# Six of sixteen attention groups transposed by the vector engine and SBUF-to-SBUF DMAs instead of the tensor engine, the last output tile in two halves, and a new written order

## The chip, the cores and the metric

The kernel runs on one core of one Trainium2 chip. A core has a tensor engine (PE, with PEld for its weight loads), a vector engine (DVE), a scalar engine (ACT), a GpSimd (POOL) and a sync engine (SP), which here issues the DMAs. SBUF is the on-chip memory, PSUM the memory into which PE writes its sums; "bank" means one 512-column fp32 buffer of PSUM. The metric is the device time of one execution in microseconds. Before the change it is 413.14 us, the median of three runs (412.8 to 413.42).

## The reference

Inputs are q, k, v of shape (8 batches, 8 heads, 576 rows, 64) and p of shape (8, 8, 32, 64), then w_in (512 x 1024), conv_w (3 x 1024) and w_out (1024 x 512).

```
p_packed = sm_attn(p, k, v)              # first attention: 32 packed rows look at 576 rows
attn     = sm_attn(q, p_packed, p_packed) # second attention: 576 rows look at the 32
x   = attn, heads side by side            # (8, 576, 512)
h   = relu(x @ w_in)
c   = conv_w[0]*h[s-1] + conv_w[1]*h[s] + conv_w[2]*h[s+1]
out = (h * sigmoid(c)) @ w_out            # (8, 576, 512)
```

sm_attn(q, k, v) is softmax(q k^T / 8) v, with each row's maximum taken off first.

## The kernel before

**Tiling.** Four heads of a batch make a group; there are 16 groups, g = 0 to 15, two for each batch. First attention of a group: eight small matmuls (L444, `big<-kT,pT`) make a 128 x 576 tile of scores (4 heads x 32 packed rows on partitions, the 576 rows in columns); DVE takes the maximum (L487, `nm`); ACT makes the exponentials `a1` (L491; the profile calls it `a`). The product with v contracts over the 576 rows, so `a1` has to be turned: five PE transposes (L498, `big<-ident,a`) of 128 x 128 into PSUM and one ACT copy (L501, `a1T<-big`) into SBUF. Then 20 pairs of small matmuls (L507, `sm<-v,a1T`) give the packed result, which ACT scales (`pb`), PE transposes (L523) and ACT copies (`ppT`). Second attention scores the 576 rows against it (L444, `big<-qT,ppT`), DVE does the softmax (L531 to L561) and leaves `a2`.

**The rest.** packed_weight multiplies the packed result into w_in beforehand (L581), so that ffn1 (L633, 12 matmuls of 288 columns for each of 8 blocks of a batch) goes from `a2` straight to h. ACT and DVE then do relu, convolution and gate (L645 to L661). ffn2 makes the 36 output tiles of 128 rows: ACT and DVE split a tile into a high and a low part (`xhi` L671, `xlo` L674), then 8 steps of 3 matmuls of 512 columns (L716) add into one PSUM bank, ACT copies it (L721, `o`) and SP stores it (L723). The bank is `fo`; for tiles 31, 33 and 35 it is `sm`, so that the last five tiles alternate.

**What sets the order.** Each stream of work (a group's attention, a tile's ffn2) is a generator that yields steps: an engine, an expected duration, the buffers taken and given. The string `ORDER` is a written-out list of stream numbers; `flow.run` takes the next step of the named stream each time. So the order of instructions on each engine's queue is fixed by `ORDER`, and every engine works its own queue strictly in that order, waiting on semaphores where data or buffers are not ready. The durations in the steps serve only to decide how many filler matmuls (L244, `idle`) PE gets in its first waits. `a1` and `a1T` have one buffer each, `o` two. DMAs of SP rotate over eight semaphores (DMAHW0 to DMAHW7): the ninth waits until the first has landed.

The steps that the change touches are in `attention(g)`: `yield Step("PE", 544, take=["big", "a1T"], give=["a1"])`, the ACT step behind it, the PE step of L507; and in `ffn2(m)`, the eight PE steps and the store.

Of the kernel before, what the change touches and what calls it, by code (L numbers as in the profile page):

```python
# [185 lines left out]
def tile_packed_attention_conv_gate(  # L186
# [11 lines left out]
    nc = tc.nc  # L198
# [20 lines left out]
    HALVED = 4  # L219

# [20 lines left out]
    def warm(n):  # L241
# [5 lines left out]
        dict(kq=3, v=2, kT=1, qT=1, big=3, sm=1, fo=1, a1=1, a1T=1, pm=2, pT=2, pb=2, ppT=5, s2=2, a2t=1, a2=4)  # L247
# [232 lines left out]

    def attention(g):
# [12 lines left out]
        yield Step("PE", 544, take=["big", "a1T"], give=["a1"], cols=1280)  # L494
        t = big().rearrange("r f s -> r (f s)")
        for si in range(SV + 1):
            rows = a1[:, : 128 * SV].rearrange("c (r s) -> c s r", s=SV)[:, si, :] if si < SV else a1[:, S - 128 :]
            nc.tensor.transpose(out=t[:, si * 128 : (si + 1) * 128], in_=rows, identity=ident)  # L498
        yield Step("ACT", 584, give=["big"])
        a1T = wk.tile([128, SV + 1, 128], F32, name="a1T", tag="a1T", bufs=1)  # L500
        nc.scalar.copy(out=a1T.rearrange("r s n -> r (s n)"), in_=t[:, : (SV + 1) * 128])  # L501
        yield Step("PE", 737, after=[("v", g)], take=["sm"], give=["a1T", "v"], cols=960, tiled=True)
        t = small()
        for si in range(SV + 1):
            r = 0 if si < SV else 128 - TAIL
            for h in range(HG):
                nc.tensor.matmul(  # L507
                    out=t[32 * h : 32 * h + 32, :D],
                    lhsT=a1T[r:, si, 32 * h : 32 * h + 32],
                    rhs=G["v"][r:, head(g, h), si, :],  # L510
                    start=si == 0,
                    stop=si == SV,
                    tile_position=(r, 32 * h),
                    skip_group_check=True,
                )
# [150 lines left out]
    split = {}  # L666

# [13 lines left out]
    def ffn2(m):  # L681
# [16 lines left out]
        for c in range(NJ):  # L698
            after = [("w", 4 + c // 2)]
            if c == 0 and m:  # L700
                after.append(("fo", m - 1))
            if c == last:
                after.append(("x", m))
            yield Step(
                "PE",
                699,
                after=after,
                take=[bank] if c == 0 else (),
                give=["x"] if c == NJ - 1 else (),
                sets=[("fo", m)] if c == NJ - 1 else None,  # L710
                cols=1536,
            )
            if c == 0:
                t = small(bank)
            for i, (x, w) in enumerate(((hi, wo_hi), (hi, wo_lo), (lo, wo_hi))):
                nc.tensor.matmul(  # L716
                    out=t, lhsT=x[:, c, :], rhs=w[:, c, :], start=c + i == 0, stop=c == NJ - 1 and i == 2
                )
        yield Step("ACT", 478, take=["o"], give=[bank])
        o = wk.tile([128, DM], F32, name="o", tag="o")  # L720
        nc.scalar.copy(out=o, in_=t)  # L721
        yield Step("SP", 728, give=["o"])
        nc.sync.dma_start(out=out.rearrange("b s f -> (b s) f")[m * 128 : (m + 1) * 128, :], in_=o)  # L723
# [57 lines left out]
```

## Time and profile before

| what | value |
|---|---|
| median of three runs | 413.14 us |
| the profiled execution, its own time | 412.19 us |
| its span, first to last instruction | 410.4 us |
| granted TensorE clock | 0.999 |
| PE busy | 399.8 us, 97% |
| DVE busy | 335.2 us, 82% |
| ACT busy | 277.5 us, 68% |
| PE transposes of `a1` (L498) | 80, in 16 groups of 5 |
| ACT copies `a1T` (L501) | 16, 700 ns each |
| output stores (L723) | 36 of 256 KB, 2.3 us from issue to landing |

Matmuls are pipelined: a row's duration runs from its start to its modelled end and overlaps the next. What a matmul costs PE is the distance from its start to the next start. A row with "x5" is five instructions merged. "[0.67 <-ACT o L721]" behind a row says that the engine was idle for 0.67 us before it, until that instruction released it.

### The profile page before, as it was taken

The numbers are of one execution on the slowest core, as the hardware profiler recorded it, in microseconds if no ns is written. First come the engines' busy times: TensorE is split into PE (matmuls) and PEld (weight loads), VectorE is DVE, ScalarE is ACT, GpSimd is POOL, SyncE is SP. The second block draws the span as 40 slices with busy tenths as digits, with TensorE's granted clock in tenths as the row PEclk, the third lists the DMA queues.
The fourth block names the chain that finished last, engine by engine and source line by source line (L and its number), as shares of the span: only waits on it lengthen the run. The fifth ranks groups of instructions, "written<-read, shape, count | busy, mean of one in ns | idle before, by whom it ended". The sixth has DMA issues, their size and how long they took to land.

```text
span 410.4 us, 8121 instructions
## 1 busy us (share of the span) xinstructions
PE 399.8 (97%) x3335; PEld 320.5 (78%) x3335; DVE 335.2 (82%) x482; ACT 277.5 (68%) x480; POOL 1.6 (0%) x13
## 2 busy tenths in 40 slices
PE   6899999999999999999999998999999999999996
PEld 5668675877868787887788786878788878887884
DVE  0599999999999999999979998888996786657220
ACT  4799999977666686677666674675755667655221
POOL 1000000000000000000000000000000000000000
PEclk9999999999999999999999999999999999999999
DMA  7999999998659919733631093710100101101021
GB/s 280 382 342 353 180 283 163 153 117 163 106 114 198 174 53 124 159 84 83 112 65 21 3 181 81 130 49 4 53 26 2 51 0 53 51 2 51 27 77 51
DMA packets 135620, 47.21 MB, mean 115 GB/s; under 512 B 119700, under 2 KB 127892, under 8 KB 135584
## 3 DMA queue, kind: packets, MB, share of 16 engines
q1 hardware_dynamic: 135552, 46.67, 52.0%
q8 instruction: 26, 0.43, 0.5%
q14 instruction: 10, 0.08, 0.1%
q0 software_dynamic: 32, 0.02, 0.0%
HBM read 37.25 MB, written 9.44 MB: 114 GB/s over the span
## 4 chain that ended last, share of the span: by engine, by line
PE 90%; DMA 4%; ACT 2%; DVE 1%; SPq 1%; issue 0%; DVEq 0%; ACTq 0%
PE fo L716 44%; PE big L633 24%; PE sm L716 4%; PE big L444 4%; PE big L581 3%; DMA v<-in_v_dram 3%; PE sm L507 3%; PE big L498 2%; PE big L328 2%; DMA q<-in_q_dram 1%; PE idle L244 1%; PE big L428 1%; SPq L405 1%; PE sm L523 1%; PE big L597 1%; ACT kT L434 0%
## 5 line engine op out<-in xcount | busy, mean ns | idle before, releaser
L716 PE MATMUL fo<-wo_hi,xhi 128*128 128x512 f32 x264 | 108.1, 410 | 0.7 <-ACT o L721 0.7
L716 PE MATMUL fo<-wo_hi,xlo 128*128 128x512 f32 x264 | 104.5, 396 | 0.0
L716 PE MATMUL fo<-wo_lo,xhi 128*128 128x512 f32 x264 | 103.9, 393 | 0.0
L651 DVE SCALAR_TENSOR_TENSOR hgt<-hbuf,cw,hgt 128x576 f32<-128x576 f32 x64 | 51.6, 810 | 16.8 <-ACT hgt L649 16.7
L645 ACT ACTIVATE hbuf<-big 128x576 f32<-128x576 f32 x64 | 41.7, 654 | 33.4 <-PE big L633 33.0
L716 PEld LDWEIGHTS fo<-wo_hi,xhi 128*128 128x128 f32 x264 | 49.6, 188 | 17.1 <-issue 3.5
L674 DVE TENSOR_TENSOR xlo<-hgt,xhi 128x1024 fp32r<-128x1024 f32 (+1 forms) x44 | 44.7, 1021 | 21.3 <-ACT xhi L671 21.0
L716 PEld LDWEIGHTS fo<-wo_hi,xlo 128*128 128x128 f32 x264 | 49.6, 188 | 12.3
L716 PEld LDWEIGHTS fo<-wo_lo,xhi 128*128 128x128 f32 x264 | 49.7, 188 | 8.6
L633 PE MATMUL big<-a2hi,ghi 128*128 128x288 f32 x256 | 55.3, 297 | 0.0
L633 PE MATMUL big<-a2hi,glo 128*128 128x288 f32 x256 | 54.3, 294 | 0.0
L633 PE MATMUL big<-a2lo,ghi 128*128 128x288 f32 x256 | 54.2, 293 | 0.0
L661 DVE SCALAR_TENSOR_TENSOR hgt<-hgt,hbuf 128x576 f32<-128x576 f32 x64 | 47.4, 749 | 7.3 <-ACT hgt L659 6.9
L655 DVE SCALAR_TENSOR_TENSOR hgt<-hbuf,cw,hgt 128x576 f32<-128x576 f32 x64 | 51.4, 811 | 0.5
L659 ACT ACTIVATE hgt<-hgt 128x576 f32<-128x576 f32 x64 | 43.1, 686 | 12.6 <-DVE hgt L655 12.2
L649 ACT ACTIVATE hgt<-hbuf,cw 128x576 f32<-128x576 f32 x64 | 49.4, 778 | 0.6
L633 PEld LDWEIGHTS big<-a2hi,ghi 128*128 128x128 f32 x256 | 43.1, 188 | 5.2 <-ACT hbuf L645 0.8
L671 ACT CAST xhi<-hgt 128x1024 fp32r<-128x1024 f32 (+1 forms) x44 | 38.9, 889 | 11.1 <-PE fo L716 6.4
L721 ACT COPY o<-fo 128x512 f32<-128x512 f32 x33 | 19.4, 587 | 33.6 <-PE fo L716 33.2
L633 PEld LDWEIGHTS big<-a2lo,ghi 128*128 128x128 f32 x256 | 40.9, 188 | 0.0
L633 PEld LDWEIGHTS big<-a2hi,glo 128*128 128x128 f32 x256 | 40.8, 188 | 0.0
L487 DVE TENSOR_REDUCE nm<-big 128x1 f32<-128x576 f32 x16 | 12.0, 752 | 10.7 <-PE big L444 10.6
(90 smaller groups left out, 503.7 us busy)
## 6 DMA issues: line engine op xcount, KB each, us to landing
out_dram<-o SPq DMA_DIRECT2D x36, 256.0 KB, 2.3
v<-in_v_dram SPq DMA_DIRECT2D x16, 512.0 KB, 5.4
k<-in_k_dram SPq DMA_DIRECT2D x48, 144.0 KB, 4.3
q<-in_q_dram SPq DMA_DIRECT2D x48, 144.0 KB, 4.2
hgt<-in_moe_w_in_dram SPq DMA_DIRECT2D x3, 1024.0 KB, 11.7
hgt<-in_moe_w_out_dram SPq DMA_DIRECT2D x3, 1024.0 KB, 8.5
hgt<-in_k_dram SPq DMA_DIRECT2D x2, 576.0 KB, 6.6
hgt<-in_q_dram SPq DMA_DIRECT2D x2, 576.0 KB, 9.3
```

The lines of the kernel that those rows point to most:

```text
L444: nc.tensor.matmul(out=o.rearrange("c (j r) -> c j r", r=NR) if by_block(g) else o, lhsT=lhs[r, 32 * i : 32 * i + 32], rhs=rhs[r, :, h, :] ...
L633: nc.tensor.matmul(out=t[:, hf, :SH], lhsT=w[:, gg, js], rhs=x[:, hf * SH : (hf + 1) * SH], start=n == 0, stop=n == 3 * NG - 1,)
L645: nc.scalar.activation(out=h[:, 1 : S + 1].rearrange("c (f s) -> c f s", f=2), in_=t[:, :, :SH], func=AF.Relu, scale=0.5)
L649: nc.scalar.activation(out=d, in_=h[:, 1 : S + 1], func=AF.Copy, scale=cw[:, NJ + j : NJ + j + 1])
L651: nc.vector.scalar_tensor_tensor(out=d, in0=h[:, 0:S], scalar=cw[:, j : j + 1], in1=d, op0=ALU.mult, op1=ALU.add)
L655: nc.vector.scalar_tensor_tensor(out=d, in0=h[:, 2 : S + 2], scalar=cw[:, 2 * NJ + j : 2 * NJ + j + 1], in1=d, op0=ALU.mult, op1=ALU.add)
L659: nc.scalar.activation(out=d, in_=d, func=AF.Tanh)
L661: nc.vector.scalar_tensor_tensor(out=d, in0=d, scalar=1.0, in1=h[:, 1 : S + 1], op0=ALU.add, op1=ALU.mult)
L671: nc.scalar.copy(out=hi[:, js, o], in_=src[:, js])
L674: nc.vector.tensor_tensor(out=lo[:, js, o], in0=src[:, js], in1=hi[:, js, o].bitcast(F32), op=ALU.subtract)
L716: nc.tensor.matmul(out=t, lhsT=x[:, c, :], rhs=w[:, c, :], start=c + i == 0, stop=c == NJ - 1 and i == 2)
L721: nc.scalar.copy(out=o, in_=t)
```

## The change

For the groups g = 10 to 15 (`MOVED = 10`) the five PE transposes and the ACT copy are replaced. DVE turns the 128 x 576 exponentials in blocks of 32 x 32 with two instructions, one over 128 x 512 and one over 128 x 64, into one of two buffers that are halves of `stage` (the buffer that held raw weights at the start). A block is then transposed in itself but lies in the wrong place: rows of head h lie on partitions 32h to 32h+31, and should lie on the partitions of their quarter q of the 576 rows. Sixteen DMAs on SP's queue, one for each q and h, each 32 rows of 160 elements (640 B a row), move them inside SBUF to `a1T`, whose layout becomes (h, s, n) for all groups. The last output tile (m = 35) is summed in two halves of 256 columns, 24 matmuls each, in the same bank `sm`, and each half is copied and stored by itself. `ORDER` is a new list throughout.

```
@@ ORDER = (
-    "003m043k0302040304033l053u040b0b05060b083v3s0106060c3k0g0j060c07063q0j050c0j3t063k070c05063k3v0e3v063t0k3t060e0k"
+    "003m3k04033s0403020403040b06080c3t063k3l063t0b0c3u010g0705050b070j3k0c3k3q0c06050e3t060e063v06060k0506063v0a0k09"
...
+    afree = [stage[:, i * (SV + 1) * 128 : (i + 1) * (SV + 1) * 128] for i in range(2)]
...
     def attention(g):
...
-        yield Step("PE", 544, take=["big", "a1T"], give=["a1"], cols=1280)
...
+        if g >= MOVED:
+            yield Step("DVE", 760, after=[("wp", 2), ("wp", 5)], take=["ad"], give=["a1"])
+            blocks = afree.pop(0)
+            moved = blocks.rearrange("r (q s n) -> r q s n", q=4, s=SV + 1)
+            main = a1[:, : 128 * SV].rearrange("c (q r s) -> c q s r", q=4, s=SV)
+            nc.vector.transpose(out=moved[:, :, :SV, :], in_=main)
+            rest = a1[:, 128 * SV :].rearrange("c (q r) -> c q r", r=32)
+            nc.vector.transpose(out=moved[:, 4 - TAIL // 32 :, SV, :], in_=rest)
+            yield Step("SP", 1100, take=["a1T"], give=["ad"], parts=4 * HG)
+            a1T = wk.tile([128, SV + 1, 128], F32, name="a1T", tag="a1T", bufs=1).rearrange("r s n -> r (s n)")
+            a1T = a1T.rearrange("r (h s n) -> r h s n", h=HG, s=SV + 1)
+            for q in range(4):
+                for h in range(HG):
+                    nc.sync.dma_start(
+                        out=a1T[32 * q : 32 * q + 32, h].rearrange("r s n -> r (s n)"),
+                        in_=moved[32 * h : 32 * h + 32, q].rearrange("r s n -> r (s n)"),
+                    )
+            afree.append(blocks)
+        else:
 ...
-                    lhsT=a1T[r:, si, 32 * h : 32 * h + 32],
+                    lhsT=a1T[r:, h, si, :],
...
     def ffn2(m):
...
-        for c in range(NJ):
+        parts = 2 if m == NTT - 1 else 1
+        for n in range(NJ * parts):
+            q, c = divmod(n, NJ)
+            fs = slice(q * DM // parts, (q + 1) * DM // parts)
...
-                    out=t, lhsT=x[:, c, :], rhs=w[:, c, :], start=c + i == 0, stop=c == NJ - 1 and i == 2
+                    out=t[:, fs], lhsT=x[:, c, :], rhs=w[:, c, fs], start=c + i == 0, stop=c == NJ - 1 and i == 2
...
-        yield Step("ACT", 478, take=["o"], give=[bank])
+        yield from store(m, fs, bank)
+
+    def store(m, fs, bank=None):
+        yield Step("ACT", 45 + (fs.stop - fs.start) * 85 // 100, after=[("fo", m, fs.start * 2 // DM)], take=["o"], give=[bank] if bank else ())
         o = wk.tile([128, DM], F32, name="o", tag="o")
+        nc.scalar.copy(out=o[:, fs], in_=sums_of[m][:, fs])
+        yield Step("SP", 100 + (fs.stop - fs.start) * 123 // 100, give=["o"])
+        nc.sync.dma_start(out=out.rearrange("b s f -> (b s) f")[m * 128 : (m + 1) * 128, fs], in_=o[:, fs])
...
+    flow.add(store(NTT - 1, slice(0, DM // 2)))
```

In the changed kernel's line numbers L445 is the scores, L490 the maximum, L502 and L504 are the two DVE transposes, L510 the sixteen DMAs, L530 the product with v, L656 ffn1, L745 ffn2's matmuls, L753 its copy, L755 its store.

Counted over the whole program PE has 50 transposes of `a` where it had 80, 48 matmuls of 256 columns for the last tile where it had 24 of 512, and 38 filler matmuls where it had 39; all other counts on PE are as before.

**DVE around the transposes of group 14.** Before, on DVE, from the maximum of group 14 on:

```order
L487 TENSOR_REDUCE nm<-big 128x1 [waits PE_49]
L655 SCALAR_TENSOR_TENSOR hgt_76<-hbuf_79,cw,hgt_76 128x576 [waits DVE_49]
L548 RECIPROCAL sm_2911<-sm_2911 128x18
L531 STREAM_TRANSPOSE s_2979<-big 128x576 [waits PE_49]
L674 TENSOR_TENSOR xlo<-hgt_77,xhi 128x1024 [waits Activation_49]
```

Now:

```order
L490 TENSOR_REDUCE nm<-big 128x1 [waits PE_49]
L684 SCALAR_TENSOR_TENSOR hgt_76<-hgt_76,hbuf_80 128x576 [waits Activation_49]
L678 SCALAR_TENSOR_TENSOR hgt_76<-hbuf_78,cw,hgt_76 128x576 [waits DVE_49]
L674 SCALAR_TENSOR_TENSOR hgt_76<-hbuf_79,cw,hgt_76 128x576
L684 SCALAR_TENSOR_TENSOR hgt_76<-hgt_76,hbuf_78 128x576 [waits Activation_49]
L678 SCALAR_TENSOR_TENSOR hgt_76<-hbuf_79,cw,hgt_76 128x576 [waits DVE_49]
L502 STREAM_TRANSPOSE stage<-a_3099 128x4x128 [waits DMAHW7_49,Activation_49]
L504 STREAM_TRANSPOSE stage<-a_3099 128x2x32
L684 SCALAR_TENSOR_TENSOR hgt_76<-hgt_76,hbuf_79 128x576 [waits Activation_49]
```

Group 14's exponentials now pass through DVE's queue a second time, behind five convolution and gate instructions of ffn1; before they went from ACT to PE without DVE. On PE, from the end of group 14's scores to its product with v, there now stand 39 matmuls of ffn2, 36 of ffn1, the product with v of group 13, the scores of group 15, one packed_weight and one small transpose.

**SP around group 11.** Before, the queue holds loads and stores alone. Now, from the end of group 10's sixteen to the first of group 11's:

```order
L510 DMA a1T<-stage 32x160 [waits DMAHW0_49]
L755 DMA out_dram<-o 128x512 [waits DMAHW1_49,Activation_49]
L510 DMA a1T<-stage 32x160 [waits DMAHW4_49,DMAHW3_49,DMAHW5_49,DMAHW2_49,DMAHW6_49,DMAHW0_49,DMAHW7_49,DVE_49,PE_49]
L510 DMA a1T<-stage 32x160 x6
L510 DMA a1T<-stage 32x160 [waits DMAHW1_49]
L510 DMA a1T<-stage 32x160 [waits DMAHW2_49,DVE_49]
```

The first DMA of group 11 waits for PE, since the one buffer `a1T` is free only when group 10's product with v is done. On PE, between group 10's product and group 11's, there stand 36 matmuls of ffn1, 24 of ffn2, two blocks of scores and two small transposes. Behind the sixteen, SP's queue goes on with two stores, four pieces of q and two loads of v.

**PE at the last tile.** Before, the last tile's 24 matmuls stand without a wait on ACT after the first of them. Now, on PE, rows 29 to 32 of the tile's 48 (the second half has begun with row 25):

```order
L745 MATMUL sm<-wo_lo,xhi 128x256
L745 MATMUL sm<-wo_hi,xlo 128x256
L745 MATMUL sm<-wo_hi,xhi 128x256 [waits Activation_49]
L745 MATMUL sm<-wo_lo,xhi 128x256
```

and on ACT the two copies:

```order
L753 COPY o<-fo 128x512 [waits DMAHW4_49,PE_49]
L753 COPY o<-sm 128x256 [waits DMAHW5_49,PE_49,Activation_49]
L753 COPY o<-sm 128x256 [waits DMAHW6_49,PE_49,Activation_49]
```

After 30 of the 48 matmuls PE waits for ACT, and PE tells its progress on this bank to ACT only with the 30th and the 48th matmul: the first half's copy stands between them on both sides.

More of the change, by code (lines that the diff above doesn't have):

```diff
@@ L219, in tile_packed_attention_conv_gate @@
     HALVED = 4
+    MOVED = 10
     cpool = ctx.enter_context(tc.tile_pool(name="consts", bufs=1))
@@ L246, in tile_packed_attention_conv_gate @@
     flow = Flow(
-        dict(kq=3, v=2, kT=1, qT=1, big=3, sm=1, fo=1, a1=1, a1T=1, pm=2, pT=2, pb=2, ppT=5, s2=2, a2t=1, a2=4)
+        dict(kq=3, v=2, kT=1, qT=1, big=3, sm=1, fo=1, a1=1, ad=2, a1T=1, pm=2, pT=2, pb=2, ppT=5, s2=2, a2t=1, a2=4)
         | dict(gw=2, h=3, x=2, o=2),
@@ L493, in attention @@
         )
-        yield Step("PE", 544, take=["big", "a1T"], give=["a1"], cols=1280)
[L495 to L500, printed above, removed]
@@ L501, in attention @@
-        nc.scalar.copy(out=a1T.rearrange("r s n -> r (s n)"), in_=t[:, : (SV + 1) * 128])
+        if g >= MOVED:
[17 more added lines that the diff above has]
+        else:
+            yield Step("PE", 544, take=["big", "a1T"], give=["a1"], cols=1280)
+            t = big().rearrange("r f s -> r (f s)")
+            for si in range(SV + 1):
+                rows = a1[:, : 128 * SV].rearrange("c (r s) -> c s r", s=SV)[:, si, :] if si < SV else a1[:, S - 128 :]
+                nc.tensor.transpose(out=t[:, si * 128 : (si + 1) * 128], in_=rows, identity=ident)
+            yield Step("ACT", 584, give=["big"])
+            a1T = wk.tile([128, SV + 1, 128], F32, name="a1T", tag="a1T", bufs=1)
+            nc.scalar.copy(out=a1T.rearrange("r s n -> r (s n)"), in_=t[:, : (SV + 1) * 128])
+            a1T = a1T.rearrange("r s (h n) -> r h s n", h=HG)
@@ L666, in tile_packed_attention_conv_gate @@
     split = {}
+    sums_of = {}
     def convert(m, js, spans):
@@ L703, in ffn2 @@
                 after.append(("x", m))
+            sets = [("fo", m, q)] * (c == NJ - 1) + [("fo", m)] * end
             yield Step(
                 "PE",
-                699,
+                699 // parts,
                 after=after,
[L708 to L711, printed above, removed]
-            )
-            if c == 0:
-                t = small(bank)
+                take=[bank] if n == 0 else (),
+                give=["x"] if end else (),
+                sets=sets,
+                cols=1536 // parts,
+            )
+            if n == 0:
+                t = sums_of[m] = small(bank)
             for i, (x, w) in enumerate(((hi, wo_hi), (hi, wo_lo), (lo, wo_hi))):
                 nc.tensor.matmul(
-                    out=t, lhsT=x[:, c, :], rhs=w[:, c, :], start=c + i == 0, stop=c == NJ - 1 and i == 2
+                    out=t[:, fs], lhsT=x[:, c, :], rhs=w[:, c, fs], start=c + i == 0, stop=c == NJ - 1 and i == 2
                 )
-        yield Step("ACT", 478, take=["o"], give=[bank])
+        yield from store(m, fs, bank)
+    def store(m, fs, bank=None):
+        yield Step("ACT", 45 + (fs.stop - fs.start) * 85 // 100, after=[("fo", m, fs.start * 2 // DM)], take=["o"], give=[bank] if bank else ())
         o = wk.tile([128, DM], F32, name="o", tag="o")
-        nc.scalar.copy(out=o, in_=t)
-        yield Step("SP", 728, give=["o"])
-        nc.sync.dma_start(out=out.rearrange("b s f -> (b s) f")[m * 128 : (m + 1) * 128, :], in_=o)
+        nc.scalar.copy(out=o[:, fs], in_=sums_of[m][:, fs])
+        yield Step("SP", 100 + (fs.stop - fs.start) * 123 // 100, give=["o"])
+        nc.sync.dma_start(out=out.rearrange("b s f -> (b s) f")[m * 128 : (m + 1) * 128, fs], in_=o[:, fs])
     for g in range(NGT):
```

57 lines of the change are left out of this document (29 added, 28 removed).

## The prediction

> **What bounds the kernel now.** First the page's busy times, then the stages.
>
> ```profile
> PE 399.8 (97%) x3335; PEld 320.5 (78%) x3335; DVE 335.2 (82%) x482; ACT 277.5 (68%) x480; POOL 1.6 (0%) x13
> ```
>
> ```profile
> 0.00:50.00 50.00, 44.86 (x560) 34.52 (x562) 35.24 (x57) 40.65 (x79) 1.58 (x13) 1.00 0.99 305
> ...
> 100.00:150.00 50.00, 50.00 (x469) 40.45 (x468) 49.28 (x76) 34.43 (x64) 0.00 (x0) 1.00 0.79 147
> 150.00:200.00 50.00, 50.00 (x427) 41.02 (x426) 48.97 (x69) 35.31 (x63) 0.00 (x0) 1.00 0.60 107
> 200.00:250.00 50.00, 49.11 (x473) 39.26 (x471) 45.98 (x67) 34.78 (x62) 0.00 (x0) 1.00 0.50 78
> 250.00:300.00 50.00, 49.73 (x358) 40.33 (x359) 45.16 (x65) 30.88 (x51) 0.00 (x0) 1.00 0.22 51
> 300.00:350.00 50.00, 50.00 (x303) 42.70 (x301) 38.57 (x53) 32.31 (x48) 0.00 (x0) 1.00 0.09 32
> ```
>
> The columns are busy PE, PEld, DVE, ACT, POOL with counts, then clock, DMA share and GB/s. From 100 us on PE never rests at full clock, so an instruction taken off its queue shortens the run, if what it waits for still comes in time. But DVE has almost as little room: 1.75 us idle between 100 and 200 us, against 20.3 us between 200 and 350. A busy PE can hide waits, so the chain of waits counts too; it gives PE the bulk, and what remains is mostly the start:
>
> ```profile
> PE 90%; DMA 4%; ACT 2%; DVE 1%; SPq 1%; issue 0%; DVEq 0%; ACTq 0%
> ```
>
> **The transposes that leave PE.** The timeline of PE around group 14's five:
>
> ```profile
> 232.29 0.74 PE L498 MATMUL big<-ident,a 128*128 128x128 f32 x5
> 232.79 0.47 PE L716 MATMUL fo<-wo_hi,xhi 128*128 128x512 f32 x1
> 233.10 0.39 PE L716 MATMUL fo<-wo_lo,xhi 128*128 128x512 f32 x1
> 233.34 0.39 PE L716 MATMUL fo<-wo_hi,xlo 128*128 128x512 f32 x1
> ```
>
> From start to start the five take 0.50 us, and the matmul behind them 0.31 instead of the 0.233 that ffn2's matmuls are apart, so a block costs PE 0.58 us. Six blocks: **-3.5 us**. ACT loses six copies of 0.70 us too; it has some 15 us idle in each 50 and sets nothing, so I count 0.
>
> **What DVE gets.** No row shows a transpose over 512 or 64 columns; the nearest are
>
> ```profile
> L555 DVE STREAM_TRANSPOSE a2t<-s 128x576 f32<-128x576 f32 x16 | 12.4, 775 | 0.1
> L567 DVE TENSOR_SCALAR rs<-sm 128x1 f32<-128x1 f32 x16 | 2.3, 146 | 1.8 <-ACT a L491 1.8
> ...
> 239.30 0.77 DVE L555 STREAM_TRANSPOSE a2t<-s 128x576 f32<-128x576 f32 x1
> 239.99 0.71 DVE L535 TENSOR_REDUCE mx<-s 128x18 f32<-128x576 f32 x1
> ```
>
> Start to start 576 columns take 0.69 us, so 512 about 0.61, and the short one at least the 0.146 of an instruction on one column: 0.76. From above, 0.69 + 0.26 by durations, 0.95. Six times: 4.6 to 5.7 us, taken as 4.6. Three groups fall after 200 us into 20 us of idle time; groups 10 to 12 (2.3 us) come in the stretch where DVE has 1.75 us. There PE has ffn2 work ready, so I count 0 and keep +2.9 us (three times 0.95) as the upper bound.
>
> **The sixteen DMAs.** No transfer inside SBUF is in the trace. The rows that bound it:
>
> ```profile
> out_dram<-o SPq DMA_DIRECT2D x36, 256.0 KB, 2.3
> ...
> q<-in_q_dram SPq DMA_DIRECT2D x48, 144.0 KB, 4.2
> ...
> 190.72 0.83 SPq L723 DMA_DIRECT2D out_dram<-o  x2
> ...
> 155.91 2.60 SPq L405 DMA_DIRECT2D q<-in_q_dram  x4
> ...
> 236.70 8.72 SPq L405 DMA_DIRECT2D q<-in_q_dram  x8
> ```
>
> Stores go out 0.42 us apart and land after 2.3; pieces of q 0.65 apart, landing after 4.2; eight pieces of q in a row 1.09 apart. So sixteen take 16 x 0.42 + 2.3 = 9.0 us at the least, 16 x 0.65 + 4.2 = 14.6 at the most if SP's queue is otherwise quiet. A piece of q is, by the code, 32 x 36 rows of 128 B, one of the new DMAs 32 rows of 640 B: it is nearer to a store, and I take 9.0. Eight take 3.4 us to issue, longer than the 2.3 to landing, so the ninth need not wait for its semaphore.
>
> Against that stands the time which PE spends elsewhere in between. Besides ffn2's 0.233 a matmul I need
>
> ```profile
> 228.03 0.65 PE big L444 x16
> 228.68 0.86 PE big L581 x16
> 230.02 0.83 PE sm L507 x40
> ...
> 238.63 0.42 PE L633 MATMUL big<-a2hi,ghi 128*128 128x288 f32 x2
> 238.89 0.42 PE L633 MATMUL big<-a2lo,ghi 128*128 128x288 f32 x2
> ```
>
> that is 0.13 us for a matmul of ffn1. The two tightest groups: between the products with v of groups 10 and 11 stand 36 ffn1 (4.7), 24 ffn2 (5.6), two score blocks (1.3) and two small transposes (0.3), 11.9 us, against 0.2 + 9.0. Group 14 has 39 ffn2 (9.1), 36 ffn1 (4.7), product (0.8), packed_weight (0.9), scores (0.7), a transpose: 16.3 us from its scores to its product. In it fall the maximum (0.7), five convolution and gate instructions of about 0.72, ACT's exponentials in their shadow, the two transposes (0.8) and 9.0 us of DMAs: about 14.3 us. The other four have 24 us or more. So **0 us**, with 2 us to spare at the tightest places; at 14.6 us a set, group 11 is late by 2.9 and group 14 by 3.6. Behind the sixteen on SP wait stores and loads of q and v, up to 9 us later than their place; one such load is late even now:
>
> ```profile
> 248.84 1.38 DVE L417 STREAM_TRANSPOSE qT<-q 128x1152 f32<-128x1152 f32 x1 [1.47 <-DMA q<-in_q_dram]
> ...
> 250.27 0.72 PE L444 MATMUL big<-qT,ppT 64*32 64x288 f32 x16 [1.17 <-DVE qT L417]
> ```
>
> PE stood for 1.17 us. The new list moves that load; between losing this stall (-1.2) and getting another like it (+1.2) I take 0. The new order of the first 50 us, where PE idles 5.1 us, has one filler less and the same work: 0, between -1 and +1.
>
> **The last tile.** The order puts the copy of the first half between PE's 30th and 31st matmul of the 48, with a wait on both sides. The trace has just such a stop, where tiles 29 and 30 share a bank:
>
> ```profile
> 371.87 0.40 PE L716 MATMUL fo<-wo_hi,xlo 128*128 128x512 f32 x1
> 372.30 0.58 ACT L721 COPY o<-fo 128x512 f32<-128x512 f32 x1 [1.99 <-PE fo L716]
> ...
> 372.94 0.50 PE L716 MATMUL fo<-wo_hi,xhi 128*128 128x512 f32 x1 [0.67 <-ACT o L721]
> ```
>
> Start of the matmul to the copy 0.43, copy 0.58, to the next matmul 0.06. A copy of 256 columns lies between the next two rows' 265 and 587 ns, by the line through them 0.37 us:
>
> ```profile
> L526 ACT COPY ppT<-sm 128x128 f32<-128x128 f32 x16 | 4.2, 265 | 1.4 <-PE sm L523 1.3
> L721 ACT COPY o<-fo 128x512 f32<-128x512 f32 x33 | 19.4, 587 | 33.6 <-PE fo L716 33.2 <-ACT xhi L671 0.4
> ```
>
> A 256-column matmul, by 0.130 at 288 and 0.233 at 512, takes 0.116, so 48 of them 5.57 against 5.60: 0; at 0.130 each it would be +0.6. The stop costs 0.43 + 0.37 + 0.06 - 0.12 = 0.74, or 0.62 if the shorter matmul also ends 0.12 sooner. At the end the copy is 0.21 shorter; the store is half as large but takes, as far as the 2.3 us of a store tells, as long to land, counted 0. The halves thus bring **+0.4 us** (0.74 - 0.21 = 0.53, or 0.62 - 0.21 - 0.12 = 0.29); without the stop they would bring -0.3.
>
> The Trainium skill, PSUM — Partial Sum Buffer, section "PSUM bank collisions raise a hardware error", says to guard PSUM by bank and quadrant and not by address, which speaks against halves in one bank: reading columns 0 to 255 beside writes to columns 256 to 511 of one bank is a collision. No run here shows a collision, but the waits in the order are those which that rule asks for. By it the tail is 0.4 us longer, by addresses alone 0.3 us shorter.
>
> **Sum.** -3.5 + 0.4 = -3.1 us on the profiled execution's 412.19, hence 409.1. The median of the runs is 0.95 above that execution (413.14): **410.0 us**, 0.76% less. About 0.2%, 0.8 us, is what can be told from no change here.
>
> **Rivals.**
> - *The DMAs come late.* If a set takes 14.6 us, PE waits 2.9 us at group 11 and 3.6 at group 14, 6.5 in all: 416.5, slower. It decides from about 13 us a set on. For it: pieces of q at 0.65 and more, and k, q and v still on the same queue. Against it: a piece of q has 36 times the rows of a new DMA. 11%.
> - *Each DMA pays its landing in turn.* Sixteen times 2.3 us is 37 us a set; with covers of 11.9 to 37 us five groups would stop PE for 10 us or more, over 460 us. Against it, eight pieces of q that land after 4.2 us each are issued within 8.72. 2%. The Trainium skill, DMA: Bandwidth & Descriptors, section "Bandwidth", asks for transfers of 1 MiB and calls those under 64 KB dominated by descriptors; each of these is 20 KB.
> - *DVE becomes the bound between 100 and 200 us* and gives back 2.9 us: 412.9, no change. For it, the 49.28 and 48.97 busy of 50; against it, ffn2 as a reserve for PE. 13%.
> - *The wait goes elsewhere better than thought*: the new list is rid of the 1.17 us stall and the tail's stop is hidden: 410.0 - 1.2 - 0.7 = 408.1. 14%.
> - The forecast, 408.8 to 411.5: 60%.
>
> That the transposes stay on PE is excluded by the counts of the order. Range: 407.8 to 412.9; above it lie the two late-DMA cases, below it little. Faster: the forecast and the fourth rival, less 0.01 for small stalls in several places, 0.73; same: DVE as the bound and that 0.01, 0.14; slower: the two DMA rivals, 0.13.
>
> **What would show it.** PE has 50 transposes of `a`, and PE busy time falls by about 3.5 us. The sixteen `a1T` DMAs take about 9 us from the first issue to the last landing; L530 shows no idle time before it in groups 10 to 15 (over 1 us there: the first rival). DVE busy grows by 4.6 to 5.7 us without new waits of PE on DVE between 100 and 200 us. Near the end PE stands once for about 0.7 us behind the copy L753 of 128 x 256. If PE's busy time falls and the span does not, a wait has taken the transposes' place.

## The result, and the profile after

The changed kernel takes 420.7 us (median of 5 runs, 419.32 to 421.28) against 413.42 of the kernel before on the same chip: a ratio of 1.017, 95% interval 1.0145 to 1.0196. The forecast was 410.0 and faster; it is slower. The profiled execution took 420.75 us, its span 418.6 (before: 412.19 and 410.4).

The page's busy times, the chain of waits and four windows of the changed kernel (columns as in the prediction):

```profile
PE 400.2 (96%) x3327; PEld 321.4 (77%) x3327; DVE 341.2 (82%) x494; ACT 275.4 (66%) x475; POOL 1.6 (0%) x13
```

```profile
PE 63%; DVE 14%; DMA 8%; ACT 6%; SPq 5%; issue 3%; DVEq 0%; ACTq 0%
```

```profile
0.00:50.00 50.00, 42.19 (x535) 32.55 (x536) 32.90 (x55) 37.67 (x72) 1.58 (x13) 0.97 0.97 301
...
150.00:200.00 50.00, 49.76 (x422) 40.84 (x421) 49.88 (x76) 34.52 (x61) 0.00 (x0) 1.00 0.40 91
200.00:250.00 50.00, 48.04 (x419) 37.77 (x419) 47.53 (x68) 31.03 (x51) 0.00 (x0) 1.00 0.58 101
250.00:300.00 50.00, 46.93 (x377) 38.00 (x377) 44.04 (x64) 30.34 (x49) 0.00 (x0) 0.97 0.28 74
```

PE's busy sum hides the 3.5 us of work that left it, partly since a matmul at half clock counts as busy for longer. The chain is the plainer sign: PE held 90% of it before and holds 63% now; SP's queue, DMA and DVE have come in. PE's own waits on the longest groups:

```profile
PE sm L530 <- DMA a1T<-stage: 3.0, 7, 1.0
PE big L429 <- DMA hgt<-in_k_dram: 2.7, 1, 2.7
PE idle L245 <- POOL ident masks.py:199: 2.5, 1, 2.5
PE sm L530 <- issue: 1.7, 1, 1.7
```

L530 is the product with v. Two of these are new: its wait for the sixteen DMAs, and 1.7 us of "issue" (time for which the profile shows no wait) at the same line. The timeline of PE at group 13 (first row) and around group 14 shows them, and what follows:

```profile
237.69 0.27 PE L530 MATMUL sm<-v,a1T 128*32 128x64 f32 x2 [0.99 <-DMA a1T<-stage]
...
255.26 0.69 PE L445 MATMUL big<-kT,pT 64*32 64x288 f32 x16
257.65 0.27 PE L530 MATMUL sm<-v,a1T 128*32 128x64 f32 x2 [1.70 <-issue]
258.19 0.30 PE L530 MATMUL sm<-v,a1T 128*32 128x64 f32 x2 [0.26 <-DMA a1T<-stage]
258.82 0.30 PE L530 MATMUL sm<-v,a1T 128*32 128x64 f32 x2 [0.34 <-DMA a1T<-stage]
259.51 0.82 PE L530 MATMUL sm<-v,a1T 128*32 128x64 f32 x30 [0.39 <-DMA a1T<-stage]
...
261.25 0.64 PE L745 MATMUL fo<-wo_hi,xhi 128*128 128x512 f32 x1 [0.38 <-ACT o L753]
261.69 0.63 PE L745 MATMUL fo<-wo_lo,xhi 128*128 128x512 f32 x1
...
264.25 0.63 PE L745 MATMUL fo<-wo_lo,xhi 128*128 128x512 f32 x1
264.68 0.49 PE L745 MATMUL fo<-wo_hi,xlo 128*128 128x512 f32 x1
```

PE takes the product piece by piece, as the DMAs land 0.6 us apart. The 1.7 us of "issue" is the same wait: the first pair of matmuls needs the thirteenth DMA of the set, the last one for head 0, which lands at 257.56 us, and PE starts at 257.65. For the 3.4 us after the product ffn2's matmuls start 0.43 us apart where 0.233 is their pace; the granted clock between 260 and 265 us is 0.66.

To place the loss, I count for each moment the **lost time**: time passed, less the matmuls that PE has started by then, each at its start-to-start time at full clock (ffn2 0.233 us, ffn1 0.130, and so on; idle matmuls count nothing). The total of those matmuls is 382.8 us before and 379.3 after. The kernels of the experiments stand beside, named there.

| lost by PE (us) at | before | after | five_dmas | pool_half | two_back | early16 | early345 |
|---|---|---|---|---|---|---|---|
| 100 us | 19.6 | 23.2 | 23.0 | 22.4 | 22.3 | 19.9 | 21.5 |
| 230 us | 20.6 | 24.6 | 24.2 | 23.7 | 23.8 | 21.4 | 22.7 |
| 270 us | 22.0 | 33.3 | 24.2 | 23.9 | 25.0 | 29.2 | 22.8 |
| 400 us | 23.8 | 34.9 | 26.2 | 25.8 | 26.5 | 30.7 | 24.8 |

So the work fell by 3.5 us as forecast; against that, 3.6 us more were lost before 100 us, where no moved group has run, and 7.3 more between 230 and 270 us (8.7 against 1.4), at groups 13 and 14.

### The profile page after: what moved, and what is told of

The parts are those of the page before. It is cut to its first block, busy times and chain, and to the rows that moved or that the text cites. A ratio compares the mean times of both kernels' runs of the same rounds, so it can differ in the third digit from the quotient of the medians.

```text
span 418.6 us, 8253 instructions
## 1 busy us (share of the span) xinstructions
PE 400.2 (96%) x3327; PEld 321.4 (77%) x3327; DVE 341.2 (82%) x494; ACT 275.4 (66%) x475; POOL 1.6 (0%) x13
## 4 chain that ended last, share of the span: by engine, by line
PE 63%; DVE 14%; DMA 8%; ACT 6%; SPq 5%; issue 3%; DVEq 0%; ACTq 0%
PE fo L745 35%; PE big L656 16%; PE sm L745 4%; SPq L510 3%; DMA stage<-in_moe_w_out_dram 3%; DMA hgt<-in_k_dram 2%; DVE hgt L674 2%; PE big L445 2%; DVE hgt L678 2%; DVE hgt L684 2%; PE big L604 2%; DMA hgt<-in_moe_w_out_dram 2%; PE sm L530 2%; PE big L429 1%; DVE xlo L698 1%
## 5 line engine op out<-in xcount | busy, mean ns | idle before, releaser
L745 PE MATMUL fo<-wo_hi,xhi 128*128 128x512 f32 x264 | 108.3, 410 | 1.2 <-ACT o L753 1.2
L745 PE MATMUL fo<-wo_hi,xlo 128*128 128x512 f32 x264 | 104.8, 397 | 0.0
L745 PE MATMUL fo<-wo_lo,xhi 128*128 128x512 f32 x264 | 104.7, 397 | 0.0
L745 PEld LDWEIGHTS fo<-wo_hi,xhi 128*128 128x128 f32 x264 | 50.1, 190 | 19.3 <-ACT o L753 4.6
L674 DVE SCALAR_TENSOR_TENSOR hgt<-hbuf,cw,hgt 128x576 f32<-128x576 f32 x64 | 50.8, 802 | 12.9 <-ACT hgt L672 12.3
L745 PEld LDWEIGHTS fo<-wo_hi,xlo 128*128 128x128 f32 x264 | 50.0, 189 | 12.3
L745 PEld LDWEIGHTS fo<-wo_lo,xhi 128*128 128x128 f32 x264 | 50.0, 189 | 8.9
L656 PE MATMUL big<-a2hi,ghi 128*128 128x288 f32 x256 | 55.4, 298 | 1.2 <-ACT hbuf L668 1.0
L656 PE MATMUL big<-a2hi,glo 128*128 128x288 f32 x256 | 54.4, 294 | 0.0
L656 PE MATMUL big<-a2lo,ghi 128*128 128x288 f32 x256 | 54.3, 294 | 0.0
L678 DVE SCALAR_TENSOR_TENSOR hgt<-hbuf,cw,hgt 128x576 f32<-128x576 f32 x64 | 50.9, 806 | 0.5
L656 PEld LDWEIGHTS big<-a2hi,ghi 128*128 128x128 f32 x256 | 43.2, 188 | 7.0 <-ACT hbuf L668 1.3
L753 ACT COPY o<-fo 128x512 f32<-128x512 f32 x33 | 19.3, 586 | 44.3 <-PE fo L745 33.9
L656 PEld LDWEIGHTS big<-a2lo,ghi 128*128 128x128 f32 x256 | 41.0, 188 | 0.0
L656 PEld LDWEIGHTS big<-a2hi,glo 128*128 128x128 f32 x256 | 40.9, 188 | 0.0
L530 PEld LDWEIGHTS sm<-v,a1T 128*32 128x32 f32 (+1 forms) x640 | 11.2, 108 | 14.8 <-issue 6.2
```

The costliest lines, as they stand in the source:

```text
L530: nc.tensor.matmul(out=t[32 * h : 32 * h + 32, :D], lhsT=a1T[r:, h, si, :], rhs=G["v"][r:, head(g, h), si, :], start=si == 0, stop=si == S ...
L656: nc.tensor.matmul(out=t[:, hf, :SH], lhsT=w[:, gg, js], rhs=x[:, hf * SH : (hf + 1) * SH], start=n == 0, stop=n == 3 * NG - 1,)
L674: nc.vector.scalar_tensor_tensor(out=d, in0=h[:, 0:S], scalar=cw[:, j : j + 1], in1=d, op0=ALU.mult, op1=ALU.add)
L678: nc.vector.scalar_tensor_tensor(out=d, in0=h[:, 2 : S + 2], scalar=cw[:, 2 * NJ + j : 2 * NJ + j + 1], in1=d, op0=ALU.mult, op1=ALU.add)
L745: nc.tensor.matmul(out=t[:, fs], lhsT=x[:, c, :], rhs=w[:, c, fs], start=c + i == 0, stop=c == NJ - 1 and i == 2)
L753: nc.scalar.copy(out=o[:, fs], in_=sums_of[m][:, fs])
```

## The experiments

Every ratio is to the kernel before, run on the same chip in the same rounds; its interval is 95%.

| kernel | us | ratio | interval |
|---|---|---|---|
| the change | 420.7 | 1.017 | 1.0145 to 1.0196 |
| five_dmas | 411.23 | 0.9961 | 0.9944 to 0.9978 |
| pool_half | 412.18 | 0.9984 | 0.9967 to 1.0002 |
| two_back | 413.71 | 1.0019 | 0.9998 to 1.0041 |
| order_only | 417.33 | 1.0113 | 1.0097 to 1.0129 |
| early16 | 416.48 | 1.0081 | 1.0050 to 1.0112 |
| early100 | 410.65 | 0.9951 | 0.9934 to 0.9968 |
| early345 | 409.90 | 0.9927 | 0.9907 to 0.9948 |
| fillers | 412.49 | 0.9990 | 0.9973 to 1.0007 |
| move_only | 453.22 | 1.0986 | 1.0942 to 1.1031 |
| move_only5 | 431.35 | 1.0435 | 1.0396 to 1.0474 |
| whole_tile | 418.04 | 1.0145 | 1.0107 to 1.0184 |
| whole5 | 410.05 | 0.9928 | 0.9900 to 0.9956 |

### The sixteen issues: five_dmas, pool_half, two_back

In the changed kernel one DMA of a set costs SP this (minimum, median, maximum in ns), and SP's timeline around group 14 reads:

```profile
L510 SPq DMA_DIRECT2D a1T<-stage x96: 514/589/1584, 149.7 to 284.7; - x96
```

```profile
a1T<-stage SPq DMA_DIRECT2D x96, 20.0 KB, 1.8
```

```profile
243.54 2.90 SPq L406 DMA_DIRECT2D q<-in_q_dram  x4
246.49 0.87 SPq L379 DMA_DIRECT2D v<-in_v_dram  x1
247.40 0.68 SPq L383 DMA_DIRECT2D v<-in_v_dram  x1
248.19 10.04 SPq L510 DMA_DIRECT2D a1T<-stage  x16
258.27 1.05 SPq L755 DMA_DIRECT2D out_dram<-o  x2
```

The sixteen start 0.63 us apart (10.04 / 16), and the last lands 1.8 us after its start. From the first start to the last landing that is 11.3 us at group 14, 11.2 to 12.3 in the six sets. (The prediction's way of adding, sixteen spacings and one landing, gives 11.9; between sixteen starts there are fifteen.) And the set begins late. DVE has the blocks of group 14 ready at 243.0:

```profile
241.77 1.09 DVE L502 STREAM_TRANSPOSE stage<-a 128x512 f32<-128x512 f32 x1
242.79 0.21 DVE L504 STREAM_TRANSPOSE stage<-a 128x64 f32<-128x64 f32 x1
```

while SP, which takes its list in order, is still at a store, four pieces of q and two loads of v: 5.2 us more. At group 13 it is the same with four pieces of k, 3.0 us. The first experiment makes the set short by fewer DMAs, through a buffer in DRAM (the cut is shortened):

```diff
-            for q in range(4):
-                for h in range(HG):
-                    nc.sync.dma_start(out=a1T[32q.., h], in_=moved[32h.., q])
+            nc.sync.dma_start(out=bounce, in_=blocks)
+            for q in range(4):
+                nc.sync.dma_start(out=a1T[32q..], in_=bounce as (q r h x), piece q)
```

> The change with a set of five DMAs in place of sixteen: one of 128 rows x 640 elements to a buffer in DRAM, then four of 32 x 4 x 160 back into a1T. Theory A (SP's 0.634 us for each issue makes a set 11.9 us and holds SP 10 us): now 0.5 + 2 + 4 x 0.63 + 2.3 = 7.3 us a set and SP held for 5; the waits at groups 13 and 14 (6.6 us) and the clock behind them (2) go all but 1 us or so: 412.5 to 415. Rival D (sets are late because the new list computes the scores late, or DVE is, not for SP's issues): 418 to 421.

411.23 us, below the 412.5 to 415 of theory A. SP's timeline of this kernel at group 14, and PE in the two windows that held the loss:

```profile
240.96 0.61 SPq L384 DMA_DIRECT2D v<-in_v_dram  x1
242.45 0.35 SPq L510 DMA_DIRECT2D bounce<-stage  x1
246.13 1.74 SPq L512 DMA_DIRECT2D a1T<-bounce  x4
247.92 0.90 SPq L757 DMA_DIRECT2D out_dram<-o  x2
```

```profile
200.00:250.00 50.00, 50.00 (x435) 39.83 (x434) 49.43 (x70) 32.45 (x54) 0.00 (x0) 1.00 0.58 118
250.00:300.00 50.00, 49.97 (x423) 39.71 (x422) 49.28 (x73) 33.80 (x55) 0.00 (x0) 1.00 0.26 68
```

SP is held for 5.4 us instead of 10, and the set takes 7.4 us from the first start to the last landing (6.4 to 7.8 in the six; 7.3 was forecast). It also begins on time: the list ahead of it is the same, but SP is through with that list at 241.57 us, before DVE is done at 242.42. In the change SP stood at group 13's set until 238.25, here until 231.83; so most of the 5.2 us by which group 14's set began late is the length of the set before it. PE does not wait once on a1T, the clock stays at 1.00, and the 8.7 us lost between 230 and 270 us are none. Fewer bytes are not the reason: it moves every byte twice. Theory A holds, rival D falls. pool_half keeps the sixteen transfers as they are and changes only who issues them:

```diff
-                    nc.sync.dma_start(
+                    (nc.gpsimd if h % 2 else nc.sync).dma_start(
```

> The change with its sixteen DMAs a set, but those of heads 1 and 3 issued by POOL's queue, which is idle then; SP issues eight. Theory A (SP's issues set the length): 8 x 0.634 + 1.8 = 6.9 us a set, if POOL issues its eight in 0.65 each, its one DMA's time; the waits at groups 13 and 14 and the clock behind them go: 420.7 - 8 = 412 to 414. Rival F (sixteen small transfers of 32 rows are slow to land, whoever issues them): still 419 to 421.

412.18 us; the windows' loss is gone here too (23.7 at 230 us, 23.9 at 270). The two queues at group 14:

```profile
241.90 4.99 SPq L510 DMA_DIRECT2D a1T<-stage  x8
```

```profile
242.38 3.91 POOL L510 DMA_DIRECT2D a1T<-stage  x8 [14.35 <-DVE stage L504]
```

Eight issues on each, side by side, with 2.1 us to landing in the median: 6.2 us for this set, 6.2 to 8.4 in the six, where 6.9 was forecast. It too begins when DVE is done. The same transfers of 32 rows are quick enough when one queue has not to issue them all, so rival F falls. The Trainium skill, DMA: Bandwidth & Descriptors, section "Issuing engines are not separate DMA queues", says that starting DMAs on several engines saves only the sequencer's time, "which is usually small relative to the DMA itself". Here that time is 10.0 us of a set of 11.3, so it is the case that the sentence's "usually" leaves out.

two_back leaves the sixteen and takes away just the two groups that were late:

```diff
-        if g >= MOVED:
+        if g >= MOVED and g not in (13, 14):
```

> The change with groups 13 and 14 given back to PE and ACT (a step whose buffer is not yet free in the list goes behind the step that frees it); groups 10, 11, 12 and 15 still move by sixteen DMAs. Theory A (only the sets of 13 and 14 are late): their waits (6.6 us) and the half clock (2) go, two blocks of transposes come back (1.2): 420.7 - 8.6 + 1.2 = 413.3. Rival I (some other group's wait, or ACT and DVE, takes their place): 416 or more.

413.71 us, against 413.3 forecast. No wait of PE on a1T is left in groups 10, 11, 12 and 15, whose sets are as long as before: 11.2 to 12.4 us hide there. So the loss between 230 and 270 us belongs to two groups of six, and rival I falls.

### The list: order_only, early16, early100, early345, fillers

order_only keeps the new list and gives all transposes back to PE. Where that step finds its PSUM buffer taken, it is put behind the step that frees it, which changes the list a little.

```diff
-    MOVED = 10
+    MOVED = 16
```

> The change's order and its halves of the last tile, but all sixteen groups keep PE's transposes and ACT's copy (a step whose buffer is not yet free in the list goes behind the step that frees it). Theory A (the sum read from the two traces: new order of the first 100 us +3.8, late sets at groups 13 and 14 +6.6, half clock after them +2, old 249 us stall gone -1.3, halves +0.35, PE work -3.5): the late sets and the clock go, the PE work returns, the early loss stays: 420.7 - 8.6 + 3.5 = 415.6, and the first 100 us still cost about 3.8 more than before. Rival B (all of the loss is the sixteen DMAs, the early loss came with them): 413 to 413.5.

417.33 us, more than both theories said. Lost by 100 us: 21.5, so 1.9 more than before and not 3.6. Another 2.8 us are lost between 150 and 180 us, where the transposes of two groups stand in places chosen for DVE and DMAs (PE waits there for ACT's exponential, 1.0 us, and for DVE, 0.3; the rest of the 2.8 was not traced). That is taken for a fault of this experiment and not of the change, which is argued and not shown. It shows that the new list alone is no gain; it doesn't price the early part. For that the first steps of the old list were put ahead of the rest of the new one; the edit stands here as the rule by which the list was made (in early100 a step whose buffer is not yet free again goes behind the step that frees it):

```diff
-    run(new)
+    run(old[:345] + [what is left of new])      # early16: on the change; early345: on five_dmas
+    run(old[:100] + [what is left of new])      # early100: on five_dmas
```

> The change with its sixteen DMAs, but the first 345 steps of the list of before. Theory A (the early loss and the late sets are separate): 420.7 - 3.0 = 417.7, still with waits at groups 13 and 14 of 5 to 7 us and, at times, half clock behind them. Rival L (the early loss sets off the late sets: SP comes late to them because the start is late): 411 to 413.

> The set of five DMAs with the first 345 steps of the list of before (up to the scores of group 6, some 82 us), then what is left of the change's list. Theory A: the whole early loss goes, 22.9 - 19.4 = 3.5 us: 411.2 - 3.5 = 407.7, and what PE has lost by 100 us is 19.4 as in the kernel before. Rival E: 410.5 to 411.5.

> The set of five DMAs (411.2) with the first 100 steps of the list of before, then what is left of the change's list. It has the load of q again ahead of the first load of w_in. Theory A (the early loss is in the list; its first part is the wait for k at 12 us and the clock of 0.85 granted after it, 1.2 us by 30 us; the rest comes between 35 and 65 us): 410.0, clock 1.00 between 10 and 20 us. Rival E (the first 65 us are bound by the loads, so that what is won early is lost again before 65 us): 411.2.

early16 gives 416.48, 0.9% under the change (forecast 417.7). PE has lost 19.9 by 100 us, as before, and between 230 and 270 us still 7.8: the two losses are separate, and rival L falls. early345 gives 409.9, 0.3% under five_dmas where 0.9% was forecast, and has lost 21.5 us by 100 us where 19.4 was forecast; early100 gives 410.65, which can't be told from five_dmas, though its clock is 1.00 between 10 and 20 us as its theory A said. In all, the early list costs 1.4 us in one comparison and 3.7 in the other. The reason that no single figure fits is in the executions: by 100 us the old start has lost 19.6, 19.6, 19.9, 21.4, 21.5 and 22.0 us in six profiled kernels (mean 20.7), the new one 21.5, 22.0, 22.3, 22.4, 23.0 and 23.2 in six (mean 22.4). This stretch, in which loads keep the DMA engines full, varies by 2 us between executions that start with the same steps. Rival E, that the loads take back what the list wins early, is thus neither shown nor excluded. By these means, the 3.6 us that the two first traces differ by are about half the list and half such variation.

A part of the variation goes with the clock that an execution was granted, which is on record for each. Six executions of five_dmas had a mean clock of 0.994 to 0.996 and took 411.6 us in the mean; three had 0.999 or 1.0 and took 410.0. In pool_half five took 412.9 and five 411.2, in two_back six 414.3 and four 413.5. All 19 executions of early100, early345 and whole5, which begin with the old list, had 0.997 or more. But so had all four of order_only, which begins with the new one, and where in an execution without a profile the clock was low is not known.

One piece of the early loss can be seen. In the new list the first load of w_in stands ahead of the first load of q, and PE then has nothing to do until group 1's k lands. First the kernel before, then the change:

```profile
9.84 1.38 PE L244 MATMUL idle<-ident 128*128 128x128 f32 x10
12.17 0.76 PE L428 MATMUL big<-ident,hgt 128*128 128x128 f32 x5 [0.96 <-DMA hgt<-in_k_dram]
```

```profile
8.15 1.61 PE L245 MATMUL idle<-ident 128*128 128x128 f32 x13
12.47 1.33 PE L429 MATMUL big<-ident,hgt 128*128 128x128 f32 x5 [2.70 <-DMA hgt<-in_k_dram]
```

After 2.70 us of rest the five transposes take 1.33 us instead of 0.76. To see whether the rest lowers the clock, fillers puts idle matmuls into it, on five_dmas:

```diff
+            if lo == 0 and name == "k" and g == 1:
+                warm(14)
```

> The set of five DMAs with 14 more of the idle 128 x 128 matmuls (0.13 us each, 1.8 us) ahead of the transposes of group 1's k, where PE stands for 2.0 us and the clock granted between 10 and 20 us is 0.83. Theory G (the clock falls because PE rests there): clock 1.00 there, and 0.5 to 1.5 us less: 410.2. Rival H (the clock falls for another reason, or the time after it is bound by the loads): 411.2.

Two windows of five_dmas, then of fillers (the granted clock stands behind POOL's busy time):

```profile
10.00:15.00 5.00, 3.00 (x22) 2.81 (x21) 2.02 (x6) 3.51 (x10) 0.00 (x0) 0.85 1.06 390
15.00:20.00 5.00, 5.00 (x79) 4.15 (x79) 1.61 (x3) 3.35 (x7) 0.00 (x0) 0.81 1.02 375
```

```profile
10.00:15.00 5.00, 4.94 (x45) 4.75 (x44) 2.69 (x7) 1.83 (x5) 0.00 (x0) 1.00 1.04 394
15.00:20.00 5.00, 5.00 (x88) 4.14 (x87) 1.32 (x2) 4.58 (x10) 0.00 (x0) 1.00 1.04 366
```

With PE kept busy the clock is 1.00, and 11 of the 12 executions of fillers had 0.999 or more, against 3 of 9 of five_dmas: it did fall because PE rested. The length of the rest fits. Of the six profiled kernels that begin with the new list, the four with a rest of 2.70, 2.40, 2.08 and 2.00 us show half clock behind it, the two with 1.85 and 1.59 us (order_only and pool_half) don't. But the time is not less (0.9990 against 0.9961). The fourteen idle matmuls are 28 records 0.11 us apart in the trace, 3.1 us and not the 1.8 that were reckoned; k landed at 12.40 us and its transposes start at 14.43, so that what the clock gave the fillers took, and this run doesn't price the clock by itself. Theory G holds for the clock alone.

### The move in the old list: move_only, move_only5

Both have the old list whole, the last tile whole, and the six groups moved, by sixteen and by five DMAs.

```diff
-ORDER = (new list)
+ORDER = (old list)
-        parts = 2 if m == NTT - 1 else 1
+        parts = 1
```

> Groups 10 to 15 moved to DVE and DMAs, but in the list of before and with the last tile whole. Theory A: first 100 us as before; PE work -3.5; a set takes 11.9 us (16 x 0.634 + 1.8) plus 1.5 for the exponential and DVE, 13.4 in all, against the 10.9 that lay between exponential and product in group 11 (late by 3) and 17.2 to 27 in the others (late by 0 to 2 in all, where loads stand ahead on SP): 413.1 - 3.5 + 3 to 5 = 413 to 415. Rival B: the DMAs cost what they cost in the changed kernel in any list: 413.1 - 3.5 + 9 to 11 = 419 to 421.

> The list of before with the last tile whole, and all six groups moved by five DMAs a set. In that list sixteen DMAs gave 453.2 us, with a set 11.9 us long and PE's product with v queued soon behind it. Theory A (PE waits there for the end of the set, so each set that is 4.6 us shorter gives that back in six groups): 453.2 - 6 x 4.6 = 425.6, some 5 less if the clock comes back to 1.00: 420 to 426. Rival J (the old list has time enough for a short set, as between exponential and product lie 10.9 to 27 us): 409 to 413. Rival K (the sets start too late on SP, their length is not the point): 440 or more.

453.22 and 431.35 us: the first is far outside what either theory said, the second between A and K. The shorter set gives back some 22 us, but 18 are left. The waits of DVE say what for; before, move_only, move_only5:

```profile
DVE qT L417 <- DMA q<-in_q_dram: 1.5, 1, 1.5
```

```profile
DVE qT L418 <- DMA q<-in_q_dram: 18.2, 2, 10.7
...
DVE kT L418 <- DMA k<-in_k_dram: 14.8, 3, 12.5
```

```profile
DVE qT L419 <- DMA q<-in_q_dram: 8.9, 2, 4.7
DVE kT L419 <- DMA k<-in_k_dram: 7.9, 3, 6.7
```

The loads of k and q stand behind the sets on SP. A set waits there for its exponential and for DVE, and everything behind it waits along: in move_only SP issues nothing from 144.1 to 152.8 us, until about the end of DVE's transposes for the first set. So in the old list the move loses with either number of DMAs (sets on a queue of their own were not tried there); my expectation had counted only the product, which waits for the set, and not the loads, which wait behind it.

### The halves: whole_tile, whole5

Both take the last tile whole again, by the second line of the diff above and with the steps of the second half taken out of the list: whole_tile on the change, whole5 on early345.

> The change with its last tile whole (one set of 24 matmuls, one copy, one store). Theory A: the stop of 0.67 us inside the tile goes, copy and tail are as before: 420.7 - 0.35 = 420.35. Rival C (the stop only moves the end's wait; halves are a gain of 0.3): 421.0.

> The set of five DMAs with the first 345 steps of the list of before (0.993 of the kernel before) and the last tile whole. Theory A (the halves cost a stop of 0.67 us and save some 0.3 at the end): 0.35 us less, 0.992 of the kernel before. Rival C (the halves save 0.3): 0.994. The stop itself (PE idle behind the copy in the middle of the last tile) must be gone from the trace.

The stop is there in the changed kernel (PE's timeline):

```profile
412.18 0.28 PE L745 MATMUL sm<-wo_hi,xlo 128*128 128x256 f32 x1
412.96 0.39 PE L745 MATMUL sm<-wo_hi,xhi 128*128 128x256 f32 x1 [0.51 <-ACT o L753]
```

0.78 us from start to start where 0.12 is the pace: 0.66 us. It is gone with the tile whole. But from PE's last matmul to the end of the span a whole tile takes 3.6, 4.2 and 4.3 us (before, whole_tile, whole5), halves 3.2 in the change and 3.1 in early345. Over all profiled kernels a whole tile takes 3.6 to 4.3 us (five, mean 3.9) and halves 3.1 to 3.9 (nine, mean 3.3), so by the means 0.6 us comes back at the end, where 0.21 to 0.33 was forecast, and stop and gain nearly cancel. In times: 0.9928 against 0.9927 for whole5 and early345, no difference that these runs can tell, and 1.0145 against 1.0170 for whole_tile, whose intervals overlap. In whole_tile's profile group 13's waits were shorter and half clock followed group 13, not 14; nothing shows that the halves had a part in that.

early345 is also, with whole5, the fastest kernel of the study, 0.7% under the kernel before (0.9907 to 0.9948): the move, with five DMAs a set, and the first 345 steps of the old list.

## Why the prediction was wrong

- **The transposes that leave PE, -3.5 us: right.** Work 382.8 to 379.3. ACT's copies cost nothing before and nothing is missed now. (That PE "never rests" from 100 us on was too strong: the prediction's own windows show 0.9 us of rest between 200 and 250 us and 0.3 between 250 and 300.)
- **What DVE gets: mis-sized, and without effect.** Forecast 0.76 to 0.95 us a group; by the timeline 1.02 + 0.13 = 1.15:

```profile
147.64 1.10 DVE L502 STREAM_TRANSPOSE stage<-a 128x512 f32<-128x512 f32 x1
148.66 0.21 DVE L504 STREAM_TRANSPOSE stage<-a 128x64 f32<-128x64 f32 x1
148.79 1.52 DVE L678 SCALAR_TENSOR_TENSOR hgt<-hbuf,cw,hgt 128x576 f32<-128x576 f32 x2
```

DVE's busy time grew by 6.0, against 4.6 to 5.7. PE still never rested on DVE between 100 and 200 us (50.00 and 49.76 busy of 50), so the rival of DVE as the bound did not come. The step that mis-sized it is "576 columns take 0.69 us, so 512 about 0.61": the row was of a transpose that reads its columns one behind the other, and the new one reads every fourth, 16 B apart. The Trainium skill, SBUF — State Buffer, section "Door 1: The DMA port swizzle (why `[64,N]` ≈ `[32,N]`)", says that accesses within one 16-byte line run at full speed and that each step to a new line costs more; the row agrees, 1.10 us against 0.77 for more columns, though no run here changes that step alone.

- **The sixteen DMAs, 0 us "with 2 us to spare": this step failed.** Two errors. The price: I took SP's 0.42 us of a store for the spacing, because a new DMA has few rows; it is 0.63, so a set is 11.3 us and not 9.0. By the prediction's own sum that alone makes group 14 late by 0.3 us (14.3 + 2.3 against 16.3). The place: I set the cover from scores to product (16.3 us at group 14) against 14.3 us of work, as if SP were free when DVE is done. SP had loads of k, q and v and a store ahead of the set, 3.0 us at group 13 and 5.2 at group 14. The set of group 14 thus ends 16.5 us after DVE (243.0 to 259.5), not 9.0. The two errors go together, since what makes SP late at group 14 is for the most part the long set of group 13 (five_dmas and pool_half, with the same list, begin group 14's set on time). At group 13, one of the four that "have 24 us or more", the same happened. I had written that stores and loads wait behind the sixteen, and had not asked what the sixteen wait behind.
- **The rival of late DMAs** (416.5, 11%) named the right mechanism with the wrong place: it put the waits at groups 11 and 14 and the limit at 13 us a set. At 11.3 us group 11 is in time, and 13 and 14 are late by their place on SP. The sign that the prediction gave for this rival, over 1 us of idle time before L530, is there (1.70, which the profile calls "issue").
- **No term for the clock.** After the waits of group 14 nine matmuls of ffn2 start 0.43 us apart: 8 x 0.196 = 1.6 us that no wait in the profile shows. In the lost time, 2.1 us between 260 and 270.
- **The new order of the first 50 us, 0 between -1 and +1: too narrow.** It cost 1.7 us by the mean of six executions against six, between 1.4 and 3.7 by the times.
- **The late load of q, 0 between -1.2 and +1.2: inside its range, at the lower end.** Its stall of 1.17 us at 250 us is gone, and no stall like it has come: five_dmas loses nothing between 230 and 270 us, where the kernel before lost 1.4.
- **The last tile, +0.4: its stop right, 0.66 against 0.62 to 0.74; its sum not confirmed.** The tail gave back 0.6 us by the means rather than 0.21 to 0.33, and whole5 and early345 can't be told apart. What reading and writing one bank without those waits would do was not tried.

The difference of the two traces adds up in lost time: -3.5 (work) + 3.6 (by 100 us) + 0.4 (to 230) + 7.3 (to 270) + 0.8 (to the end, the stop in it) - 0.4 (behind PE's end) = 8.2 us, the spans' 418.6 - 410.4.

## What to carry to other kernels

Work taken off the bounding engine and given to DMAs is paid on the queue that issues them: count issues times the spacing of the nearest DMA of the same shape, add what stands ahead of them on that queue at that moment (the last such set included), and ask what waits behind. Where that doesn't fit, fewer DMAs (even with twice the bytes) or a second queue were each worth about 2% here. And take a first look at a stretch bound by loads in more than one execution before a list of steps is blamed for 2 us of it.

## What the runs showed of the hardware that was not expected

- A DMA of 32 rows of 640 B inside SBUF holds SP for 0.59 us (median of 96), a store of 128 rows of 2 KB for 0.36 (median of 36 in the kernel before); the read of 32 x 4 rows of 640 B from DRAM comes every 0.44 us. Rows and bytes don't rank the time to issue.
- POOL issued the same DMAs in 0.49 us each (3.91 for 8), quicker than SP.
- Half clock follows waits that are each short. At group 14 the single rests of PE were 1.70, 0.26, 0.34 and 0.39 us. The Trainium skill, TensorE: Matmul & The Clock Gate, section "HAM oscillation — how this bites in real kernels", gives the rule of no rest over about 3.4 us; here rests of 2.7 us in all within 4 us were enough, so the measurement is stricter than that rule. After group 13's waits (0.99, 0.39, 0.31 and 0.27) the clock stayed at 1.00 in this execution, while in whole_tile half clock followed the shorter ones of group 13 (0.51, 0.39, 0.30 and 0.28). So neither the longest rest nor their sum decides, and what does is not shown here.
